# Seven output stores of an attention-and-gate kernel, issued by SyncE instead of ScalarE

## The chip, the core and the metric

The kernel runs on one core of a Trainium2 chip. The metric is the device time of one execution in microseconds (us), the median of several runs. The engines are named as in the profile: PE is TensorE (PEld its weight loads), ACT is ScalarE, DVE is VectorE, POOL is GpSimd, SP is SyncE. SP does no arithmetic here: it only issues DMA transfers. A name with a q behind it (SPq, ACTq) is the instruction queue of that engine, in which DMA-issuing instructions stand. DMA-issuing instructions are not counted as busy time of their engine.

## What is computed

Two steps, for 8 batches, 8 heads, 576 positions and a head width of 64. The first is causal attention in blocks of 64 (a position sees its own block and all earlier ones); the second gates a linear layer with a causal convolution over 5 positions and multiplies by an output matrix.

```python
scores = scale * np.matmul(q, k.transpose(0, 1, 3, 2))
scores = np.where(block_i >= block_j, scores, -1e9)
attn = softmax(scores)
x = (attn @ v).transpose(0, 2, 1, 3).reshape(B, S, H * D)      # 8 x 576 x 512
gate = sigmoid(sum over k of conv_w[k] * x shifted by 4 - k)
out = (gate * (x @ w_val)) @ w_out                             # 8 x 576 x 512, fp32
```

## The kernel before

**Order written by hand.** The whole program is a list of words, `PLAN`, and a loop (L643) that reads them one after the other and calls one small function for each. A word is `name/arguments/engine/PSUM banks`: `E/20.0/A` is the function `E` with arguments 20 and 0 on ACT, `S/20.0/P/6+7` is `S` on PE into PSUM banks 6 and 7. The engine letters are P (PE), A (ACT), V (DVE), G (POOL) and S (SP). No scheduler reorders them: on each engine the instructions stand in the order of the words. A layer below adds the semaphores: what an instruction waits for follows from the tiles that it reads and writes.

**The attention.** A unit `k` is four heads' worth of q or k, a pair `p` (0 to 31) is two heads. `lQ` loads q or k into the fp32 tiles `st`, `lv` and `lvt` load v into `vs` and `vts`; SP issues all of these loads. `c` casts a unit to fp16, `T` transposes it on PE, `Te` copies the transposed unit out of PSUM into `qkT`. `S` multiplies q by k into two PSUM banks, `E` (ACT, L395) takes the exponential of them into the tile `pt`, `mka` and `mkb` (POOL, L415) set the masked corner of `pt` to zero, `cv` casts v (POOL or DVE) into `v16`, `A` multiplies `pt` by v, `N` (DVE) divides by the sum of the row into `x16`. `SL`, `EL`, `AT` and `NT` do the same for the last 64 positions. `X` and `XT` transpose the result and `Xe`, `XTe` copy it into `xt`.

**The gate.** `C` is the convolution on PE, `CS` (ACT) its tanh, `V` the product with `w_val`, `Ve` (DVE) multiplies the two into `gv`, `O` multiplies 128 rows of `gv` by `w_out` into one PSUM bank.

**The output.** `Oe` copies such a 128 x 512 block from PSUM into one of six buffers `osb` (`NOSB`, L129), on ACT (L228) or on DVE (L230). `Od` (L614, L615) stores it to `out`, 256 KB in one DMA. The buffers are used in turn in the order of the `Oe` words, so the copy number n + 6 waits until the store of copy n has landed.

```python
    DMA = {"S": nc.sync, "A": nc.scalar}                       # L224

    def Od(u, t, eng, bank=None):                              # L614
        DMA[eng].dma_start(out=rows(u, t), in_=outs[u, t][0:128])
```

The letter in an `Od` word therefore says which engine issues the store: `S` puts it among the loads in SP's queue, `A` among the exponentials and copies in ACT's queue. Of the 35 stores of `osb`, SP issues 24 and ACT 11. Every DMA reports its landing on one of eight semaphores, which are dealt out in turn and used again; before a DMA is issued, its issuer waits until the DMA that had this semaphore before has landed. The listings below call them DMAHW0 to DMAHW7.

Of the kernel before, what the change touches and what calls it, by code (L numbers as in the profile page):

```python
# [65 lines left out]
C/4/P/0+1+4+5 T/22/P/2+3 CS/4.1/A CS/4.0/A O/1.4/P/6 S/20.2/P/4+5 E/20.2/A Te/22/V Oe/1.4/V  # L66
lQ/14.1.0/S Od/0.5/S lv/20.0/S lQ/12.1.1/S AT/4/P/7 S/21.0/P/0+1 T/23/P/2+3 S/21.1/P/4+5 E/21.0/A
E/21.1/A O/1.1/P/6 Oe/1.1/A NT/4/V Te/23/V A/16/P/0+1 S/23.2/P/2+3 S/22.2/P/4+5 E/22.2/A A/17/P/6+7
E/23.2/A cv/22/G mkb/18/G lQ/14.0.0/S lv/21.1/S lQ/13.0.1/S Od/1.4/A lQ/13.0.0/S lQ/13.1.1/S
lv/23.1/S lv/20.1/S lv/23.0/S lv/27.1/S c/25/G cvt/6/G c/24/G N/16/V N/17/V V/4.3/P/0 A/19/P/4+5  # L70
Ve/4.3/V S/20.0/P/6+7 X/8/P/2+3 E/20.0/A Xe/8/A A/18/P/0+1 N/19/V XT/4/P/4 O/1.2/P/5 N/18/V XTe/4/V
S/23.0/P/6+7 SL/5/P/2+3 S/20.1/P/0+1 Oe/1.2/V X/9/P/4 V/4.2/P/5 E/23.0/A EL/5/A Xe/9/V Ve/4.2/V
# [1 line left out]
T/24/P/2+3 S/22.0/P/0+1 S/23.1/P/6+7 E/22.0/A E/23.1/A lQ/13.1.0/S lvt/5/S Od/1.0/S lQ/14.0.1/S  # L74
cv/21/G lv/26.1/S lv/24.0/S mkb/23/G cv/20/G mkb/22/G mka/21/G mkb/21/G mka/20/G mka/23/G c/29/G
Ve/5.3/V Ve/4.0/V Te/24/V O/1.3/P/5 V/5.2/P/4 Oe/1.3/V S/22.1/P/2+3 E/22.1/A T/26/P/0+1 S/24.2/P/6+7
E/24.2/A Od/0.7/A V/5.0/P/5 Ve/5.2/V Te/26/V A/20/P/2+3 cvt/5/G mka/22/G c/27/G S/24.1/P/0+1
S/24.0/P/6+7 E/24.1/A E/24.0/A Ve/5.0/V cv/23/G N/20/V V/4.1/P/5 lv/25.1/S lQ/15.1.1/S lQ/15.1.0/S
lv/26.0/S Od/1.1/S lv/25.0/S lv/27.0/S Ve/4.1/V V/5.1/P/4 S/25.0/P/0+1 E/25.0/A T/27/P/2+3
S/25.2/P/6+7 AT/5/P/5 A/21/P/0+1 E/25.2/A Ve/5.1/V Te/27/V NT/5/V N/21/V S/25.1/P/2+3 A/22/P/4+5  # L80
O/1.6/P/6 E/25.1/A N/22/V S/27.2/P/2+3 T/29/P/0+1 S/27.1/P/4+5 Te/29/V Oe/1.6/A E/27.2/A E/27.1/A
O/2.1/P/6 XT/5/P/7 XTe/5/A Oe/2.1/V mkb/24/G mkb/25/G cv/26/G lv/28.1/S lQ/15.0.1/S lQ/15.0.0/S
lv/31.1/S lv/24.1/S Od/1.2/S Od/2.1/A A/23/P/2+3 X/10/P/0+1 S/27.0/P/4+5 E/27.0/A O/1.5/P/7 N/23/V
Xe/10/V S/26.2/P/2+3 X/11/P/0+1 S/26.1/P/4+5 cv/25/V Xe/11/V O/2.2/P/6 E/26.2/A Oe/1.5/A E/26.1/A
C/6/P/0+1+2+3 cv/27/V Oe/2.2/V c/30/V cv/24/V c/28/G c/31/G Od/1.3/S lv/30.0/S Od/2.2/S lv/30.1/S
lv/28.0/S Od/1.5/S lv/31.0/S lvt/7/S Od/1.6/S CS/6.0/A CS/6.1/A T/28/P/4+5 Te/28/V V/6.0/P/6
# [9 lines left out]
mkb/29/G Ve/7.0/V S/30.1/P/0+1 S/30.0/P/2+3 S/31.2/P/4+5 E/30.1/A E/30.0/A mka/30/G E/31.2/A  # L96
mkb/31/G V/7.2/P/7 V/7.3/P/6 A/29/P/0+1 Ve/7.2/V A/30/P/2+3 Ve/7.3/V O/3.0/P/4 A/28/P/6+7 N/30/V
N/29/V N/28/V A/31/P/2+3 N/31/V O/2.8/P/5 AT/7/P/6 X/15/P/2+3 X/14/P/0+1 NT/7/V Xe/14/V O/2.4/P/7
XT/7/P/6 XTe/7/V Oe/2.4/V Xe/15/A Oe/3.0/A Oe/2.8/A Od/2.8/A C/8/P/0+1+2+3 C/9/P/4+5+6+7 CS/8.0/A
Od/2.5/A CS/9.1/A Od/2.6/A CS/8.1/A Od/2.4/A CS/9.0/A Od/3.0/S Od/2.3/S V/9.2/P/0 V/8.3/P/1  # L100
V/8.0/P/6 V/8.1/P/7 V/8.2/P/2 V/9.3/P/3 V/9.0/P/4 V/9.1/P/5 Ve/8.0/V Ve/8.3/V Ve/8.1/V Ve/8.2/V
O/3.3/P/2 O/3.1/P/1 Ve/9.2/V Ve/9.1/V Ve/9.3/V Ve/9.0/V Oe/3.1/V Oe/3.3/A Od/3.3/A Od/3.1/S
O/3.4/P/2 Oe/3.4/A Od/3.4/A O/3.2/P/4 Oe/3.2/V OL/0/P/2 OL/1/P/3 OLe/0/V Od/3.2/A OLe/1/V OLd/0/A
# [593 lines left out]
```

## Time and profile before

| what | us |
| --- | --- |
| median of 3 runs | 179.41 |
| lowest and highest of these runs | 178.64 and 180.15 |
| the profiled execution, its own time | 180.11 |
| the span of the profiled execution | 178.2 |
| PE busy in that span | 164.5 |
| ACT busy | 136.8 |
| DVE busy | 129.1 |
| POOL busy | 71.6 |

The span runs from the first to the last instruction of the profiled execution; 1.91 us of its own time lie around it. All times in the views are counted from the start of the span. In a row of the timeline stand the start, the length, the engine, the line of the kernel, the operation, the tile written and the tile read, the number of instructions of that kind in a row (x2), and in brackets how long the engine stood idle before it and which engine, by the profile, ended that wait.

### The profile page before, as it was taken

How to read it: one execution, taken by the hardware profiler on the slowest of the kernel's cores; microseconds unless marked ns; L12 is line 12 of the kernel's file. 1: busy time of each engine (PE TensorE's matmuls, PEld its weight loads, DVE VectorE, ACT ScalarE, POOL GpSimd, SP SyncE). 2: the span in 40 equal slices, each digit the busy share in tenths (PEclk: the TensorE clock that was granted, in tenths of full speed). 3: DMA queues.
4: the chain of work that ended last, by engine and by line, in shares of the span. 5: the costliest groups of instructions: out<-in, count | busy, mean ns of one | idle time of the engine just before them, and what ended most of it. 6: DMA issues, size and time to landing. Idle time of an engine off the chain costs nothing.

```text
span 178.2 us, 7667 instructions
## 1 busy us (share of the span) xinstructions
PE 164.5 (92%) x3292; PEld 95.2 (53%) x3292; DVE 129.1 (72%) x238; ACT 136.8 (77%) x161; POOL 71.6 (40%) x149
## 2 busy tenths in 40 slices
PE   7688789989999999999999969999999999999991
PEld 2233565565454765666546635565553755755450
DVE  4478997576879889985768847988994846744730
ACT  3388999985799889998999498887887699065142
POOL 6233664827557557573373810654103053000000
PEclk9999999999999999999999999999999999999999
DMA  6999979999989999999999999157476200045085
GB/s 190 332 353 266 266 204 298 216 311 310 349 179 304 297 295 246 352 332 339 280 257 302 264 299 276 67 132 227 136 185 212 81 4 4 0 165 197 21 307 204
DMA packets 53692, 40.35 MB, mean 226 GB/s; under 512 B 39701, under 2 KB 39957, under 8 KB 53658
## 3 DMA queue, kind: packets, MB, share of 16 engines
q1 hardware_dynamic: 51930, 36.85, 71.8%
q10 hardware_dynamic: 1728, 3.02, 4.5%
q8 instruction: 25, 0.41, 1.1%
q14 instruction: 9, 0.07, 0.1%
HBM read 30.42 MB, written 9.44 MB: 224 GB/s over the span
## 4 chain that ended last, share of the span: by engine, by line
PE 68%; DVE 12%; DMA 5%; issue 4%; ACT 4%; SPq 3%; POOL 3%; POOLq 0%; ACTq 0%; DVEq 0%
PE PS L135 60%; PE PS L139 7%; DVE qkT L230 3%; DMA st<-in_k_dram 3%; DVE gv L577 2%; DMA out_dram<-osb 2%; DVE qk L230 2%; ACT pt L395 2%; POOL pt L415 1%; DVE x L447 1%; DVE w_val L230 1%; SPq L264 1%; ACT th L559 1%; SPq L258 1%; DVE xt L230 1%
## 5 line engine op out<-in xcount | busy, mean ns | idle before, releaser
L395 ACT ACTIVATE pt<-PS 128x1024 f16<-128x1024 f32 x96 | 93.0, 1030 | 9.0 <-PE PS L135 8.0
L230 DVE COPY qkT<-PS 128x1152 f16<-128x1152 f16 (+1 forms) x29 | 38.7, 1334 | 6.8 <-PE PS L139 6.7
L415 POOL MEMSET pt<- 64x256 f16 x64 | 20.9, 348 | 46.5 <-ACT pt L395 36.6
L577 DVE SCALAR_TENSOR_TENSOR gv<-th,PS 128x112 f16<-128x112 f32 (+4 forms) x64 | 26.1, 449 | 17.7 <-PE PS L135 14.9
L135 PE MATMUL PS<-qkT 64*128 64x64 f16 (+4 forms) x384 | 36.1, 277 | 2.8 <-ACT pt L395 1.4
L135 PE MATMUL PS<-xt,w_val 128*128 128x464 f16 x160 | 35.7, 360 | 0.5 <-ACT osb L228 0.4
L135 PE MATMUL PS<-w_out,gv 128*128 128x512 f16 (+1 forms) x148 | 35.6, 374 | 0.0
L135 PEld LDWEIGHTS <-pt 128*128 128x128 f16 (+1 forms) x960 | 27.7, 102 | 8.6 <-issue 4.0
L135 PE MATMUL PS<-v,pt 128*128 128x65 f16 (+1 forms) x896 | 30.7, 194 | 1.3 <-DVE x L447 0.8
L230 POOL CAST qk<-st 128x1152 f16<-128x1152 f32 (+1 forms) x23 | 25.7, 1128 | 13.8 <-DMA st<-in_q_dram 4.9
L447 DVE TENSOR_TENSOR x<-PS,rc 128x512 f16<-128x512 f32 x32 | 22.1, 692 | 1.3 <-DVE rc L446 0.2
L135 PEld LDWEIGHTS <-qkT 64*128 64x128 f16 x384 | 13.1, 94 | 17.7 <-issue 12.6
L135 PEld LDWEIGHTS <-w_val 128*128 128x128 f16 x160 | 13.9, 97 | 15.8 <-issue 3.9
L559 ACT ACTIVATE th<-PS 128x928 f32<-128x928 f32 x20 | 17.8, 946 | 5.1 <-PE PS L135 5.1
L230 POOL CAST v<-vs 128x512 f16<-128x512 f32 x26 | 15.9, 617 | 11.8 <-issue 6.8
L135 PEld LDWEIGHTS <-gv 128*128 128x128 f16 x148 | 12.7, 98 | 13.3 <-issue 2.2
L228 ACT COPY osb<-PS 128x512 f32<-128x512 f32 x18 | 10.5, 590 | 10.9 <-PE PS L135 7.7
L139 PE MATMUL PS<-ident,qk 64*128 64x64 f16 x576 | 13.7, 190 | 3.1 <-DVE qk L230 2.2
L139 PEld LDWEIGHTS <-qk 64*128 64x128 f16 x576 | 11.5, 95 | 9.0 <-DVE qk L230 3.3
L135 PE MATMUL PS<-xt,DG 32*32 32x464 f16 x800 | 13.1, 358 | 0.9 <-DVE xt L230 0.4
L230 DVE COPY osb<-PS 128x512 f32<-128x512 f32 x17 | 11.7, 686 | 2.5 <-PE PS L135 1.9
L230 DVE COPY xt<-PS 128x1024 f16<-128x1024 f16 (+1 forms) x15 | 8.7, 583 | 5.6 <-PE PS L139 5.6
(49 smaller groups left out, 103.5 us busy)
## 6 DMA issues: line engine op xcount, KB each, us to landing
st<-in_q_dram SPq DMA_DIRECT2D x32, 288.0 KB, 5.4
st<-in_k_dram SPq DMA_DIRECT2D x32, 288.0 KB, 5.2
vs<-in_v_dram SPq DMA_DIRECT2D x64, 128.0 KB, 5.1
out_dram<-osb SPq DMA_DIRECT2D x24, 256.0 KB, 3.4
out_dram<-osb ACTq DMA_DIRECT2D x11, 256.0 KB, 2.4
vts<-in_v_dram SPq DMA_DIRECT2D x8, 128.0 KB, 4.9
gv<-in_moe_w_val_dram SPq DMA_DIRECT2D x2, 512.0 KB, 6.9
osb<-in_moe_w_out_dram SPq DMA_DIRECT2D x2, 512.0 KB, 5.7
```

The costliest lines, as they stand in the source:

```text
L135: made.append(nc.tensor.matmul(out=out, lhsT=lhsT, rhs=rhs, start=start, stop=stop, skip_group_check=True))
L139: made.append(nc.tensor.transpose(out=out, in_=in_, identity=identity))
L228: i = nc.scalar.copy(out=out, in_=in_)
L230: i = (nc.vector if eng == "V" else nc.gpsimd).tensor_copy(out=out, in_=in_)
L258: DMA[eng].dma_start(out=rot(vs, p)[0:128, 0:4, h, 0:64], in_=v[b, 4 * w + 2 * h + r, 0:512, 0:64].rearrange("(c p) d -> p c d", p=128))
L264: DMA[eng].dma_start(out=vts[b % 2][32:96, 0:8, 0:64], in_=v[b, 0:8, 512:576, 0:64].rearrange("h s d -> s h d"))
L395: made.append(nc.scalar.activation(out=rot(pts, p)[0:128, 0:2, 512 * t:512 * t + 512], in_=both(take("S", p, t)), func=AF.Exp, bias=0.0, s ...
L415: nc.gpsimd.memset(rot(pts, p)[64:128, 0:2, a:a + 2 * step].rearrange("p h (t s) -> p h t s", t=2)[:, :, :, 0:64], 0.0)
L447: made.append(nc.vector.tensor_tensor(out=rot(x16, p // 2)[0:128, 0:4, 0:2, p % 2].rearrange("p i h d -> p h i d"), in0=r[:, :, :, 0:64], ...
L559: made.append(nc.scalar.activation(out=rot(ths, n)[0:128, 2 * i:2 * i + 2], in_=both(take("C", n, i))[:, :, 0:RUN], func=AF.Tanh, bias=0.0 ...
L577: made.append(nc.vector.scalar_tensor_tensor(out=gv[0:128, x, a - 4 * i:e - 4 * i], in0=rot(ths, n)[0:128, x, a - o:e - o], scalar=1.0, in ...
```

## The change

The engine letter of seven `Od` words is changed from `A` to `S`: `Od/1.4`, `Od/0.7` and `Od/2.1` in mid-run, and `Od/2.8`, `Od/2.5`, `Od/2.6` and `Od/2.4` shortly before the last two convolutions. Their places in the list of words stay as they are, and nothing else is changed. Five `A` letters stay: `Od/3.3`, `Od/3.4`, `Od/3.2`, `Od/2.7` and `OLd/0`. Two of the changed lines:

```diff
-E/23.2/A cv/22/G mkb/18/G lQ/14.0.0/S lv/21.1/S lQ/13.0.1/S Od/1.4/A lQ/13.0.0/S lQ/13.1.1/S
+E/23.2/A cv/22/G mkb/18/G lQ/14.0.0/S lv/21.1/S lQ/13.0.1/S Od/1.4/S lQ/13.0.0/S lQ/13.1.1/S
-Od/2.5/A CS/9.1/A Od/2.6/A CS/8.1/A Od/2.4/A CS/9.0/A Od/3.0/S Od/2.3/S V/9.2/P/0 V/8.3/P/1
+Od/2.5/S CS/9.1/A Od/2.6/S CS/8.1/A Od/2.4/S CS/9.0/A Od/3.0/S Od/2.3/S V/9.2/P/0 V/8.3/P/1
```

PE's, DVE's and POOL's instructions stand as before; ACT loses seven DMA issues and SP gains them. The first place is ACT's queue around `Od/1.4`. The rows are `E/22.2` and `E/23.2` (into `pt_4` and `pt_5`), the store, `E/20.0` (into `pt_2`) and `Xe/8` (into `xt`); in brackets stand the semaphores that each row waits for.

```order
 L395 ACTIVATE pt_4_110<-PS_63 128x2x512 [waits PE_49,Activation_49,Pool_49]
 L395 ACTIVATE pt_5_111<-PS_63 128x2x512 [waits DVE_49,PE_49]
-L615 DMA out_0_dram<-osb_127 128x512 [waits DMAHW4_49]
 L395 ACTIVATE pt_2_108<-PS_63 128x2x512 [waits DVE_49,PE_49]
 L228 COPY xt_122<-PS_63 128x2x512 [waits PE_49]
```

The store, and with it a wait for the DMA semaphore DMAHW4, is gone from between `E/23.2` and `E/20.0`. The second place is SP's queue at the same words. Before, the rows are `lQ/13.0.1`, `lQ/13.0.0` (into `st_2`), `lQ/13.1.1` (into `st_3`), `lv/23.1`, `lv/20.1`, `lv/23.0` and `lv/27.1`.

```order
L251 DMA st_2_79<-in_q_dram 128x576 [waits DMAHW7_49]
L251 DMA st_2_79<-in_q_dram 128x576 [waits DMAHW0_49]
L251 DMA st_3_80<-in_k_dram 128x576 [waits DMAHW1_49]
L258 DMA vs_3_86<-in_v_dram 128x4x64 [waits DMAHW2_49,Pool_49]
L258 DMA vs_0_83<-in_v_dram 128x4x64 [waits DMAHW3_49]
L258 DMA vs_3_86<-in_v_dram 128x4x64 [waits DMAHW4_49]
L258 DMA vs_2_85<-in_v_dram 128x4x64 [waits DMAHW5_49,Pool_49]
```

After the change the store `Od/1.4` stands second in the same stretch of SP's queue:

```order
L251 DMA st_2_79<-in_q_dram 128x576 [waits DMAHW7_49]
L615 DMA out_0_dram<-osb_127 128x512 [waits DMAHW0_49,DVE_49]
L251 DMA st_2_79<-in_q_dram 128x576 [waits DMAHW1_49]
L251 DMA st_3_80<-in_k_dram 128x576 [waits DMAHW2_49]
L258 DMA vs_3_86<-in_v_dram 128x4x64 [waits DMAHW3_49,Pool_49]
L258 DMA vs_0_83<-in_v_dram 128x4x64 [waits DMAHW4_49]
L258 DMA vs_3_86<-in_v_dram 128x4x64 [waits DMAHW5_49]
L258 DMA vs_2_85<-in_v_dram 128x4x64 [waits DMAHW6_49,Pool_49]
```

The store brings a wait for DVE (its copy `Oe/1.4`) into SP's queue, and the loads behind it move on by one semaphore. The third place is the end of SP's queue, from `Od/1.8` (first row) over `Od/3.0` before, or `Od/2.8` after, to `Od/3.1` and `OLd/1`.

```order
 L615 DMA out_0_dram<-osb_127 128x512 [waits DMAHW1_49,DVE_49]
 L615 DMA out_0_dram<-osb_127 128x512 [waits DMAHW2_49,Activation_49]
-L615 DMA out_0_dram<-osb_127 128x512 [waits DMAHW4_49]
+L615 DMA out_0_dram<-osb_127 128x512 [waits DMAHW3_49,DVE_49]
+L615 DMA out_0_dram<-osb_127 128x512 [waits DMAHW4_49,DVE_49]
+L615 DMA out_0_dram<-osb_127 128x512 [waits DMAHW5_49,DVE_49]
+L615 DMA out_0_dram<-osb_127 128x512 [waits DMAHW6_49]
+L615 DMA out_0_dram<-osb_127 128x512 [waits DMAHW7_49]
 L615 DMA out_0_dram<-osb_127 128x512 [waits DMAHW1_49,DVE_49]
 L628 DMA out_0_dram<-olast_1_76 128x256 [waits DMAHW4_49,DVE_49]
```

The four late stores now go out one behind the other ahead of `Od/3.0` and `Od/2.3`, and the four rows that ACT had between its tanh instructions are gone.

More of the change, by code (lines that the diff above doesn't have):

```diff
@@ L76 @@
 Ve/5.3/V Ve/4.0/V Te/24/V O/1.3/P/5 V/5.2/P/4 Oe/1.3/V S/22.1/P/2+3 E/22.1/A T/26/P/0+1 S/24.2/P/6+7
-E/24.2/A Od/0.7/A V/5.0/P/5 Ve/5.2/V Te/26/V A/20/P/2+3 cvt/5/G mka/22/G c/27/G S/24.1/P/0+1
+E/24.2/A Od/0.7/S V/5.0/P/5 Ve/5.2/V Te/26/V A/20/P/2+3 cvt/5/G mka/22/G c/27/G S/24.1/P/0+1
 S/24.0/P/6+7 E/24.1/A E/24.0/A Ve/5.0/V cv/23/G N/20/V V/4.1/P/5 lv/25.1/S lQ/15.1.1/S lQ/15.1.0/S
@@ L82 @@
 O/2.1/P/6 XT/5/P/7 XTe/5/A Oe/2.1/V mkb/24/G mkb/25/G cv/26/G lv/28.1/S lQ/15.0.1/S lQ/15.0.0/S
-lv/31.1/S lv/24.1/S Od/1.2/S Od/2.1/A A/23/P/2+3 X/10/P/0+1 S/27.0/P/4+5 E/27.0/A O/1.5/P/7 N/23/V
+lv/31.1/S lv/24.1/S Od/1.2/S Od/2.1/S A/23/P/2+3 X/10/P/0+1 S/27.0/P/4+5 E/27.0/A O/1.5/P/7 N/23/V
 Xe/10/V S/26.2/P/2+3 X/11/P/0+1 S/26.1/P/4+5 cv/25/V Xe/11/V O/2.2/P/6 E/26.2/A Oe/1.5/A E/26.1/A
@@ L98 @@
 N/29/V N/28/V A/31/P/2+3 N/31/V O/2.8/P/5 AT/7/P/6 X/15/P/2+3 X/14/P/0+1 NT/7/V Xe/14/V O/2.4/P/7
-XT/7/P/6 XTe/7/V Oe/2.4/V Xe/15/A Oe/3.0/A Oe/2.8/A Od/2.8/A C/8/P/0+1+2+3 C/9/P/4+5+6+7 CS/8.0/A
-Od/2.5/A CS/9.1/A Od/2.6/A CS/8.1/A Od/2.4/A CS/9.0/A Od/3.0/S Od/2.3/S V/9.2/P/0 V/8.3/P/1
+XT/7/P/6 XTe/7/V Oe/2.4/V Xe/15/A Oe/3.0/A Oe/2.8/A Od/2.8/S C/8/P/0+1+2+3 C/9/P/4+5+6+7 CS/8.0/A
+Od/2.5/S CS/9.1/A Od/2.6/S CS/8.1/A Od/2.4/S CS/9.0/A Od/3.0/S Od/2.3/S V/9.2/P/0 V/8.3/P/1
 V/8.0/P/6 V/8.1/P/7 V/8.2/P/2 V/9.3/P/3 V/9.0/P/4 V/9.1/P/5 Ve/8.0/V Ve/8.3/V Ve/8.1/V Ve/8.2/V
```

## The prediction

> **What bounds the kernel now.** I read the page first, then the windows, the waits of one window, and the timelines of the engines around each of the seven stores.
>
> ```profile
> span 178.2 us, 7667 instructions
> PE 164.5 (92%) x3292; PEld 95.2 (53%) x3292; DVE 129.1 (72%) x238; ACT 136.8 (77%) x161; POOL 71.6 (40%) x149
> vs<-in_v_dram SPq DMA_DIRECT2D x64, 128.0 KB, 5.1
> ```
>
> PE is busy for 92% of the span, so PE is the bound. A saving counts here only where it removes idle time of PE, or of an engine for which PE waits. The windows show where PE is idle between the first and the last moved store:
>
> ```profile
> core 0: us, PE busy (x) PEld busy (x) DVE busy (x) ACT busy (x) POOL busy (x), PEclk, DMA share, GB/s
> 100.00:105.00 5.00, 3.20 (x60) 1.95 (x58) 2.84 (x7) 2.34 (x4) 2.46 (x7) 1.00 1.04 259
> 105.00:125.00 20.00, 20.00 (x406) 11.60 (x402) 16.91 (x26) 16.99 (x20) 7.74 (x12) 1.00 0.66 191
> 125.00:138.00 13.00, 12.64 (x263) 6.60 (x263) 10.27 (x19) 10.67 (x15) 2.05 (x7) 1.00 0.59 173
> 138.00:158.00 20.00, 20.00 (x481) 12.89 (x480) 14.33 (x36) 13.63 (x17) 4.32 (x11) 1.00 0.07 22
> ```
>
> PE is busy in every microsecond of 100 to 158 but for two holes: 1.80 us (5.00 less 3.20) between 100 and 105, and 0.36 us between 125 and 138. The granted clock is 1.00 throughout, so clock plays no part. `Od/1.4` stands in the first hole. ACT and PE there:
>
> ```profile
> 98.08 1.94 ACT L395 ACTIVATE pt<-PS 128x1024 f16<-128x1024 f32 x2 [0.26 <-PE PS L135]
> 102.15 0.43 ACTq L615 DMA_DIRECT2D out_dram<-osb  x1
> 102.68 1.02 ACT L395 ACTIVATE pt<-PS 128x1024 f16<-128x1024 f32 x1 [2.66 <-PE PS L135]
> 103.60 1.01 ACT L228 COPY xt<-PS 128x1024 f16<-128x1024 f16 x1
> 104.49 1.04 ACT L395 ACTIVATE pt<-PS 128x1024 f16<-128x1024 f32 x1
> 105.40 0.62 ACT L410 ACTIVATE pt<-PS 128x512 f16<-128x512 f32 x1
> ```
>
> ```profile
> 99.99 0.39 PE L135 MATMUL PS<-qkT 64*128 64x512 f16 x2
> 100.22 0.40 PE L139 MATMUL PS<-ident,x 64*128 64x64 f16 x16
> 101.63 1.03 PE L135 MATMUL PS<-w_out,gv 128*128 128x512 f16 x4
> 103.75 0.39 PE L135 MATMUL PS<-qkT 64*128 64x512 f16 x2 [1.09 <-ACT pt L395]
> 104.65 0.51 PE L135 MATMUL PS<-qkT 64*128 64x64 f16 x12 [0.51 <-ACT xt L228]
> 106.43 0.37 PE L135 MATMUL PS<-xt,DG 32*32 32x464 f16 x2
> ```
>
> ACT is done with `E/23.2` at 100.02 and starts `E/20.0` at 102.68, 2.66 us later. The profile names PE as the releaser, but the scores that `E/20.0` reads (`S/20.0`, the PE row at 99.99) were complete at 100.38. What stands between is the store at 102.15. Its listing waits for nothing but DMAHW4, and the load that SP issued with DMAHW4 in that stretch is `lv/23.0`:
>
> ```profile
> 96.82 0.55 SPq L258 DMA_DIRECT2D vs<-in_v_dram  x1
> ```
>
> Issued at 96.82, with the median landing time of v loads of 5.1 us, it lands at an estimated 101.9, next to the store's 102.15. So I read the hole as this: the store, whose data were ready at 95.05 (DVE row below), held ACT's queue until an unrelated load had landed, and `E/20.0` and `Xe/8` behind it were late for PE, which needs their PSUM banks for `S/23.0` and `SL/5`.
>
> **The change, part by part.** *Store `Od/1.4` off ACT.* `E/20.0` can start at about 100.42, when its scores are there, instead of 102.68; `Xe/8` 0.92 later (102.68 to 103.60), at 101.34 to 102.35. PE then reaches `S/23.0` behind `O/1.2` with its bank free. The two idle times are 1.09 and 0.51, together 1.60. A row's modelled end overlaps its successor by 0.16 (99.99 plus 0.39 against 100.22), so each hole hides another 0.16: 1.60 + 0.32 = 1.92. `S/23.0` would run at 102.50 and `SL/5` at 102.73 instead of 104.65. Next in line is the convolution `C/5`, at 106.43 less 1.92 = 104.51. It needs `EL/5`: `E/23.0` starts when `S/23.0` is complete, 102.9, `EL/5` 0.91 behind it (104.49 to 105.40), done at 104.45. That just fits; nothing of the 1.92 is lost here, but no more than 1.92 can be had either. Lower bound 0.53, the store's own issue and the gap behind it (102.15 to 102.68); upper bound 2.66, ACT's whole idle time. I take 1.92, because it comes from PE's own rows, the bound engine's. From 105 on PE is without a hole but for 0.36, so the gain is carried to the end if nothing else comes too late.
>
> *Stores `Od/0.7` and `Od/2.1` off ACT.*
>
> ```profile
> 112.72 1.02 ACT L395 ACTIVATE pt<-PS 128x1024 f16<-128x1024 f32 x1 [0.27 <-PE PS L135]
> 113.34 0.34 ACTq L615 DMA_DIRECT2D out_dram<-osb  x1
> 123.66 0.34 ACTq L615 DMA_DIRECT2D out_dram<-osb  x1
> 124.13 1.02 ACT L395 ACTIVATE pt<-PS 128x1024 f16<-128x1024 f32 x1 [0.36 <-PE PS L135]
> ```
>
> The issue at 113.34 lies under an exponential that runs to 113.74, past its own end at 113.68: zero. Behind the issue at 123.66 ACT has 0.36 of idle time; its exponential waited for `S/27.0`, so at most 0.1 is the store's. I take zero.
>
> *The four late stores off ACT.*
>
> ```profile
> 158.12 0.34 ACTq L615 DMA_DIRECT2D out_dram<-osb  x1
> 158.56 0.94 ACT L559 ACTIVATE th<-PS 128x928 f32<-128x928 f32 x1 [0.47 <-PE PS L135]
> 160.25 6.44 PE L135 MATMUL PS<-xt,w_val 128*128 128x464 f16 x32
> ```
>
> ACT's tanh waits there for a convolution of PE, and PE runs on from 160.25 for 6.44 us without a gap. Between 0 and 0.47 (the idle time at 158.56); I take zero, since the bound engine does not wait for ACT.
>
> *The same stores on SP.* Each costs 0.33 to 0.43 of SP's queue, some 2.6 in all, and what its waits cost the loads behind it.
>
> ```profile
> 93.11 0.98 SPq L251 DMA_DIRECT2D st<-in_q_dram  x2
> 94.37 0.68 DVE L230 COPY osb<-PS 128x512 f32<-128x512 f32 x1
> 101.67 0.62 POOL L230 CAST v<-vs 128x512 f16<-128x512 f32 x1 [0.51 <-DMA vs<-in_v_dram]
> 102.34 0.81 POOL L415 MEMSET pt<- 64x256 f16 x3
> 106.99 0.31 POOL L415 MEMSET pt<- 64x256 f16 x1 [3.84 <-ACT pt L395]
> 109.46 1.15 ACT L228 CAST qk<-st 128x1152 f16<-128x1152 f32 x1
> 113.88 0.77 PE L135 MATMUL PS<-v,pt 128*128 128x65 f16 x20
> ```
>
> `Od/1.4` reaches the head of SP's queue at 93.6, after the first of the two q loads, and its copy ends at 95.05: SP is held 1.4, plus 0.43 of issue, and the loads behind are issued up to 1.9 later. They also share the DMA engines (share 1.00) with 256 KB more, 1.0 us at the 259 GB/s of that window, so they land at most 2.9 late, and not below zero. The one cast that already waits for such a load is `cv/20` at 101.67. Behind it POOL needs 0.62 and 0.81 and then stands idle for 3.84, until `E/20.1` is done. That comes 1.6 earlier in the changed kernel, which leaves 2.2 of cover against 2.9: at worst one memset is 0.7 late, and its reader `A/20` stands at 113.88, some 6 us behind. Cost zero, at worst some tenths. `c/26` on ACT (109.46), the next reader of these loads, has time for over 5 us of lateness: `lQ/13.0.0` is issued at about 95.5 and c/26 comes at 107.5.
>
> ```profile
> 107.21 9.99 SPq L258 DMA_DIRECT2D vs<-in_v_dram  x3
> 121.26 1.70 SPq L615 DMA_DIRECT2D out_dram<-osb  x2
> 125.53 0.39 SPq L258 DMA_DIRECT2D vs<-in_v_dram  x1
> 132.13 0.62 SPq L615 DMA_DIRECT2D out_dram<-osb  x1
> 135.62 0.58 ACT L228 COPY osb<-PS 128x512 f32<-128x512 f32 x1 [1.18 <-DMA out_dram<-osb]
> ```
>
> `Od/0.7` joins the queue ahead of the stretch at 107.21, in which SP waits for most of 9.99 us for a buffer anyway: covered. `Od/2.1` stands between the two stores at 121.26; its copy is ready when ACT issues it now (123.66), so SP is held to about 124.1, ahead of the load at 125.53 that waits for DVE in any case: covered by 1.4. The late four are followed by stores only, whose buffers are copied into again behind PE's 6.44 us from 160.25: covered.
>
> The sum is −1.92. Against the profiled execution that is 180.11 − 1.92 = 178.2, a span of 176.3. The profiled execution is 0.70 above the median of the runs shown, so the median becomes 179.41 − 1.92 = 177.5.
>
> [...] ACT's idle time holds 2.13 us of waiting ahead of the store and 0.53 of issue. [...]
>
> **The rivals.**
>
> *Issue time alone.* If the profile is right that PE released `E/20.0`, the wait stays and only 0.53 goes: 178.9. For it speaks the releaser named; against it that PE's row had ended 2.3 us earlier. Chance 0.08.
>
> *The gain is partly given back.* PE has no slack to hide a late input in 105 to 158, and `C/5` comes out within 0.1 of its last input. If a cast, a DVE copy or a load becomes the bound there, some 0.6 to 1.2 of the 1.92 is left: 178.2 to 178.8. Against it: every engine waits for PE, not PE for them, in these rows. Chance 0.20.
>
> *Slower: SP's queue becomes the bound at `Od/1.6`.* ACT's copy at 135.62 already waits 1.18 for the store that SP issues at 132.13, and PE's hole of 0.36 hangs on it. Each microsecond by which SP comes later to this store is a microsecond of PE. This starts when `Od/2.1` holds SP past the load at 125.53, so when it is over 1.4 later than I reckon; to end slower it must cost over 1.92 more than that. With 3 us in its place: 179.41 − 1.92 + 3 = 180.5. Chance 0.10, since mishaps of that size upstream (loads landing 5 us late) count here too.
>
> **How the numbers follow.** My forecast, the hole at 100 to 105 closed, has 0.62. About 1% (1.8 us) is what a measurement of this kernel can tell from no change, and 177.5 lies just beyond it: 0.46 of the 0.62 is faster by over 1%, since half of its spread of 1.5 to 2.7 and the chance of a longer wait in other executions lie there. The rest, 0.16, the issue alone and the partial gain (0.28), and none of the slower case, are within 1%: 0.44. Slower by over 1% is 0.10. The range runs from ACT's whole 2.66 (176.7) to no gain at all (179.4), and leaves the slower case and a little on the other side out.
>
> **What would show it.** In the changed profile the windows should give PE near 5.0 of 5.0 in 100 to 105; `E/20.0` should start within 0.5 of `E/23.2`'s end; the store `Od/1.4` should be issued by SP at about 95.1, with a wait for DVE's copy; the 0.36 at 125 to 138 should stay; the rest of PE should be the same rows about 1.9 earlier. I am wrong if ACT still idles over 2 us there, if PE shows a new hole behind a load or behind POOL, or if the wait for `Od/1.6` grows.

## The result, and the profile after

| | median us (lowest to highest) | executions |
|---|---|---|
| before, beside it | 181.03 (178.64 to 185.0) | 22 |
| changed | 178.67 (176.57 to 181.54) | 22 |

The ratio of changed to before is 0.9888, 95% interval 0.9855 to 0.9921: about 1.1% faster. The prediction of −1.92 on 179.41 is a ratio of 0.9893. The changed median is 1.2 us above the predicted 177.5 and inside its range; before itself measured 1.6 above the median that the prediction started from. The ratios, here and below, leave out executions that took over 1.5% longer than the fastest of their kernel, while the medians and ranges are of all executions. The execution that was profiled for the changed kernel is its longest (181.54 us): it had lost 2.56 us ahead of the change, where PE stood idle for 1.81 us and then ran at half its clock for 3.4 us. So I compare inside the stretch of the change, and with a second profile of the same kernel further down. First the head of that page, and its windows. The columns are as in the prediction, with a stretch of the half clock (30 to 40) added:

```profile
span 179.5 us, 7673 instructions
PE 165.8 (92%) x3292; PEld 95.5 (53%) x3292; DVE 128.9 (72%) x238; ACT 137.1 (76%) x161; POOL 72.0 (40%) x149
```

```profile
core 0: us, PE busy (x) PEld busy (x) DVE busy (x) ACT busy (x) POOL busy (x), PEclk, DMA share, GB/s
30.00:40.00 10.00, 9.33 (x171) 4.82 (x170) 5.97 (x10) 8.99 (x11) 6.50 (x12) 0.85 0.82 231
100.00:105.00 5.00, 4.77 (x95) 3.39 (x94) 3.96 (x9) 4.10 (x5) 2.58 (x6) 1.00 0.99 237
105.00:125.00 20.00, 19.98 (x414) 11.65 (x412) 16.94 (x28) 16.76 (x20) 9.04 (x16) 1.00 0.72 203
125.00:138.00 13.00, 12.56 (x262) 6.47 (x261) 10.53 (x18) 10.51 (x13) 2.05 (x7) 1.00 0.62 185
138.00:158.00 20.00, 20.00 (x420) 12.59 (x418) 14.38 (x35) 13.64 (x17) 4.32 (x11) 1.00 0.11 36
```

Between 100 and 105 PE is busy for 4.77 of 5.00 us, where it was 3.20. The 0.36 between 125 and 138 has stayed, as 0.44. The granted clock of 0.85 between 30 and 40 is where time was lost; the moved stores all come later. ACT around the place, in the changed kernel (start, length, instruction, and in brackets the idle time before it with its releaser):

```profile
100.64 1.94 ACT L395 ACTIVATE pt<-PS 128x1024 f16<-128x1024 f32 x2 [0.27 <-PE PS L135]
103.22 1.02 ACT L395 ACTIVATE pt<-PS 128x1024 f16<-128x1024 f32 x1 [0.64 <-PE PS L135]
...
108.75 1.78 ACT L559 ACTIVATE th<-PS 128x928 f32<-128x928 f32 x2 [0.44 <-PE PS L135]
```

The last row begins with `CS/5.1`. Before, that was:

```profile
107.79 0.94 ACT L559 ACTIVATE th<-PS 128x928 f32<-128x928 f32 x1 [0.86 <-PE PS L135]
```

`E/22.2` with `E/23.2` comes 2.56 us later than before (98.08 to 100.64), and `CS/5.1` only 0.96 later (107.79 to 108.75): 1.60 us were won between them. The idle time before `E/20.0` is 0.64 instead of 2.66, a little over the 0.5 that the prediction named. The end of the span keeps what was won here, less 0.3 us at a second place that comes and goes (told further down): 179.5 against 178.2 is 1.3 later.

The second profile of the changed kernel, taken with the experiments, has a span of 175.9 and stands at before's times up to this place, so that its rows compare directly. ACT, and then PE:

```profile
98.10 1.94 ACT L395 ACTIVATE pt<-PS 128x1024 f16<-128x1024 f32 x2 [0.27 <-PE PS L135]
100.45 1.02 ACT L395 ACTIVATE pt<-PS 128x1024 f16<-128x1024 f32 x1 [0.41 <-PE PS L135]
...
104.03 0.59 ACT L410 ACTIVATE pt<-PS 128x512 f16<-128x512 f32 x1
105.98 1.78 ACT L559 ACTIVATE th<-PS 128x928 f32<-128x928 f32 x2 [0.44 <-PE PS L135]
```

```profile
100.01 0.39 PE L135 MATMUL PS<-qkT 64*128 64x512 f16 x2
101.64 1.03 PE L135 MATMUL PS<-w_out,gv 128*128 128x512 f16 x4
102.59 0.72 PE L135 MATMUL PS<-qkT 64*128 64x512 f16 x14
104.67 1.27 PE L135 MATMUL PS<-xt,DG 32*32 32x464 f16 x80
```

`S/20.0` is at 100.01 (99.99 before). `S/23.0` and `SL/5`, which began at 103.75 and 104.65 and had idle time before each, are one row at 102.59 without any, and `C/5` begins at 104.67 instead of 106.43. That is 1.78 us on PE, since `S/20.0` itself is 0.02 later. On ACT, from 98.10 to 105.98 are 7.88 us where 98.08 to 107.79 were 9.71: 1.83 less.

### The profile page after: what moved, and what is told of

It is laid out like the page before. It is cut to its first block, busy times and chain, and to the rows that moved or that the text cites. A ratio compares the mean times of both kernels' runs of the same rounds, so it can differ in the third digit from the quotient of the medians.

```text
span 179.5 us, 7673 instructions
## 1 busy us (share of the span) xinstructions
PE 165.8 (92%) x3292; PEld 95.5 (53%) x3292; DVE 128.9 (72%) x238; ACT 137.1 (76%) x161; POOL 72.0 (40%) x149
## 3 DMA queue, kind: packets, MB, share of 16 engines
q10 hardware_dynamic: 720, 1.18, 1.8%
## 4 chain that ended last, share of the span: by engine, by line
PE 68%; DVE 9%; ACT 6%; DMA 6%; issue 4%; POOL 3%; SPq 2%; POOLq 0%; ACTq 0%; DVEq 0%
PE PS L135 60%; PE PS L139 7%; ACT pt L395 4%; DVE qkT L230 3%; DMA st<-in_k_dram 3%; DMA out_dram<-osb 3%; DVE gv L577 2%; ACT th L559 2%; POOL pt L415 1%; DVE x L447 1%; DVE qk L230 1%; SPq L258 1%; SPq L251 1%; ACT osb L228 1%; POOL qk L230 1%
## 5 line engine op out<-in xcount | busy, mean ns | idle before, releaser
L415 POOL MEMSET pt<- 64x256 f16 x64 | 21.5, 358 | 46.6 <-ACT pt L395 36.8
L135 PEld LDWEIGHTS <-DG 32*32 32x32 f16 x800 | 9.4, 89 | 5.8 <-issue 4.0
```

The lines of the kernel that those rows point to most:

```text
L135: made.append(nc.tensor.matmul(out=out, lhsT=lhsT, rhs=rhs, start=start, stop=stop, skip_group_check=True))
L415: nc.gpsimd.memset(rot(pts, p)[64:128, 0:2, a:a + 2 * step].rearrange("p h (t s) -> p h t s", t=2)[:, :, :, 0:64], 0.0)
```

## The experiments

The theory to be tested: on ACT the store `Od/1.4` waits at the head of an in-order queue for a semaphore that an unrelated load still holds, and that wait, not the issue, costs PE 1.8 us. The rivals are the issue time alone (PE, as the profile says, releases `E/20.0`), and, for what is left of the time, that SP's queue with one store more makes its loads late.

### One store alone, and the other six alone

The first kernel moves `Od/1.4` alone from ACT to SP; the edit is against before:

```diff
-E/23.2/A cv/22/G mkb/18/G lQ/14.0.0/S lv/21.1/S lQ/13.0.1/S Od/1.4/A lQ/13.0.0/S lQ/13.1.1/S
+E/23.2/A cv/22/G mkb/18/G lQ/14.0.0/S lv/21.1/S lQ/13.0.1/S Od/1.4/S lQ/13.0.0/S lQ/13.1.1/S
```

> Only Od/1.4 is issued by SyncE; the other six stores stay on ScalarE. Theory (the one store's semaphore wait is the whole effect): as the full change, 1.5 to 2.1 us under the kernel before, ratio about 0.989; ACT's idle time ahead of E/20.0 falls from 2.66 to under 0.7 us, PE idle between E/20.0's scores and the convolution C/5 falls from 1.6 to 0.2 us or less. Rival (all seven count, each by its issue of 0.34 to 0.43): about 0.5 us under the kernel before.

Measured: 177.97 us (177.41 to 178.38, 9 executions), ratio to before 0.9903, interval 0.9868 to 0.9938. The rows are those of the changed kernel:

```profile
97.95 1.94 ACT L395 ACTIVATE pt<-PS 128x1024 f16<-128x1024 f32 x2 [0.26 <-PE PS L135]
100.30 1.02 ACT L395 ACTIVATE pt<-PS 128x1024 f16<-128x1024 f32 x1 [0.41 <-PE PS L135]
105.85 1.78 ACT L559 ACTIVATE th<-PS 128x928 f32<-128x928 f32 x2 [0.44 <-PE PS L135]
```

From 97.95 to 105.85 are 7.90 us: one store carries the whole gain. The opposite edit, again against before, moves the other six and leaves `Od/1.4` on ACT:

```diff
-E/24.2/A Od/0.7/A V/5.0/P/5 Ve/5.2/V Te/26/V A/20/P/2+3 cvt/5/G mka/22/G c/27/G S/24.1/P/0+1
+E/24.2/A Od/0.7/S V/5.0/P/5 Ve/5.2/V Te/26/V A/20/P/2+3 cvt/5/G mka/22/G c/27/G S/24.1/P/0+1
...
-lv/31.1/S lv/24.1/S Od/1.2/S Od/2.1/A A/23/P/2+3 X/10/P/0+1 S/27.0/P/4+5 E/27.0/A O/1.5/P/7 N/23/V
+lv/31.1/S lv/24.1/S Od/1.2/S Od/2.1/S A/23/P/2+3 X/10/P/0+1 S/27.0/P/4+5 E/27.0/A O/1.5/P/7 N/23/V
...
-XT/7/P/6 XTe/7/V Oe/2.4/V Xe/15/A Oe/3.0/A Oe/2.8/A Od/2.8/A C/8/P/0+1+2+3 C/9/P/4+5+6+7 CS/8.0/A
-Od/2.5/A CS/9.1/A Od/2.6/A CS/8.1/A Od/2.4/A CS/9.0/A Od/3.0/S Od/2.3/S V/9.2/P/0 V/8.3/P/1
+XT/7/P/6 XTe/7/V Oe/2.4/V Xe/15/A Oe/3.0/A Oe/2.8/A Od/2.8/S C/8/P/0+1+2+3 C/9/P/4+5+6+7 CS/8.0/A
+Od/2.5/S CS/9.1/A Od/2.6/S CS/8.1/A Od/2.4/S CS/9.0/A Od/3.0/S Od/2.3/S V/9.2/P/0 V/8.3/P/1
```

> The other six stores are issued by SyncE, Od/1.4 stays on ScalarE. Theory: no gain; the hole at E/20.0 stays. By the order the store shares its semaphore now with the load one place further on (lv/27.1 instead of lv/23.0), which lands some 0.5 us later, so the hole may grow by about 0.5: time equal to the kernel before or up to 0.6 us above it. Rival (the six others carry part of the gain): 0.5 to 1.5 us under the kernel before, with the hole at E/20.0 unchanged.

Measured: 181.39 us (178.69 to 185.38, 12), ratio 1.0025, interval 0.9974 to 1.0077. ACT:

```profile
97.96 1.94 ACT L395 ACTIVATE pt<-PS 128x1024 f16<-128x1024 f32 x2 [0.26 <-PE PS L135]
101.23 0.37 ACTq L615 DMA_DIRECT2D out_dram<-osb  x1
101.71 1.02 ACT L395 ACTIVATE pt<-PS 128x1024 f16<-128x1024 f32 x1 [1.81 <-PE PS L139]
106.83 1.78 ACT L559 ACTIVATE th<-PS 128x928 f32<-128x928 f32 x2 [0.86 <-PE PS L135]
```

The hole stays and nothing is gained: the six are worth nothing, as reckoned. The hole is 1.81 us and not as long as before's 2.66; I had expected it to grow. In this kernel the store shares its semaphore with `lv/27.1` instead of `lv/23.0`, and SP issued that load at 96.36, earlier than before's `lv/23.0` at 96.82, and it landed faster: 4.85 us from issue to landing (96.36 to 101.21), as against 5.30 (96.82 to 102.12). So in these two profiles the length of the hole follows the load, not the store. From 97.96 to 106.83 this execution needs 8.87 us, 0.84 less than before's 9.71; the median of the 12 doesn't show that as a gain.

### The store stays on ACT, at two other places

If the wait counts and the issue does not, a store on ACT is harmless where its semaphore is free, and harmful where it is not. Both kernels move only the one word, on before, and all stores of ACT stay on ACT. First behind `E/20.1`:

```diff
-E/23.2/A cv/22/G mkb/18/G lQ/14.0.0/S lv/21.1/S lQ/13.0.1/S Od/1.4/A lQ/13.0.0/S lQ/13.1.1/S
+E/23.2/A cv/22/G mkb/18/G lQ/14.0.0/S lv/21.1/S lQ/13.0.1/S lQ/13.0.0/S lQ/13.1.1/S
...
-C/5/P/2+3+6+7 E/20.1/A CS/5.1/A CS/5.0/A T/25/P/0+1 Te/25/V V/5.3/P/5 V/4.0/P/4 c/26/A mkb/20/G
+C/5/P/2+3+6+7 E/20.1/A Od/1.4/A CS/5.1/A CS/5.0/A T/25/P/0+1 Te/25/V V/5.3/P/5 V/4.0/P/4 c/26/A mkb/20/G
```

> As the kernel before, all seven stores on ScalarE, but Od/1.4 stands behind E/20.1, four ACT operations later. There it shares its semaphore with the load lv/24.0, issued 6 us later than lv/23.0. Theory (the wait counts, wherever it stands): E/20.0 starts at once, the hole moves to the tanh of C/5 (CS/5.1), which starts 2 us or more late, until lv/24.0 has landed; PE stands idle there for 1.5 us or more, and the time is within 0.5 us of the kernel before. Rival (what the profile names, PE, or only the place of the issue counts): no hole of over 0.6 us on ACT at either place, 0.5 to 1.9 us under the kernel before.

Measured: 179.6 us (177.75 to 183.09, 12), ratio 0.9947, interval 0.9896 to 0.9999. ACT, then PE's longest wait between 96 and 160 (total, times, longest):

```profile
100.47 1.02 ACT L395 ACTIVATE pt<-PS 128x1024 f16<-128x1024 f32 x1 [0.41 <-PE PS L135]
...
108.38 0.38 ACTq L615 DMA_DIRECT2D out_dram<-osb  x1
108.81 1.78 ACT L559 ACTIVATE th<-PS 128x928 f32<-128x928 f32 x2 [3.24 <-DMA vs<-in_v_dram]
```

```profile
PE PS L139 <- ACT th L559: 2.6, 1, 2.6
```

The hole has gone from before `E/20.0` (0.41) and stands behind `E/20.1`, 3.24 us long, and here the profile itself names a load of v as the releaser of a tanh that reads nothing of v. The time was expected within 0.5 us of before; by the ratio it is 1.0 us under it. In the list of words that load, `lv/24.0`, stands behind the store: the layer deals the semaphores out in an order of its own, not in that of the words. The same kernel once more:

> The kernel with Od/1.4 behind E/20.1 on ScalarE once more: its profile showed ACT held 3.24 us by the load that shares the store's semaphore, PE idle 2.6 us, and a granted clock of 0.50 for 3.4 us behind that, but its median was 0.5% under the kernel before. Theory: the wait is real in every execution and the half clock only in some; the profile shows a hole of 2 to 3.5 us on ACT ahead of CS/5.1 again, and where the clock stays at 1.0 the rows behind the hole come within 1 us of those of the kernel before. Rival (the hole was an accident of one execution): no hole over 1 us.

Measured: 180.25 us (177.8 to 184.51, 13), ratio 1.0082, interval 1.0026 to 1.0138. The hole was there again, and longer than the 2 to 3.5 us expected:

```profile
111.19 0.37 ACTq L615 DMA_DIRECT2D out_dram<-osb  x1
111.62 1.78 ACT L559 ACTIVATE th<-PS 128x928 f32<-128x928 f32 x2 [6.09 <-DMA vs<-in_v_dram]
```

PE waited 5.5 us for it, and behind that its clock was at 0.50 for 3.4 us again (by the windows 0.80 in 110 to 115 and 0.93 in 115 to 125), so what happens at the full clock wasn't seen. The wait is where the theory puts it, but its length differs between executions, from 3.24 to 6.09 us, and the two times, 0.9947 and 1.0082, differ by more than their intervals allow. The second place is two exponentials further, behind `E/23.1` (against before):

```diff
-E/23.2/A cv/22/G mkb/18/G lQ/14.0.0/S lv/21.1/S lQ/13.0.1/S Od/1.4/A lQ/13.0.0/S lQ/13.1.1/S
+E/23.2/A cv/22/G mkb/18/G lQ/14.0.0/S lv/21.1/S lQ/13.0.1/S lQ/13.0.0/S lQ/13.1.1/S
...
-T/24/P/2+3 S/22.0/P/0+1 S/23.1/P/6+7 E/22.0/A E/23.1/A lQ/13.1.0/S lvt/5/S Od/1.0/S lQ/14.0.1/S
+T/24/P/2+3 S/22.0/P/0+1 S/23.1/P/6+7 E/22.0/A E/23.1/A Od/1.4/A lQ/13.1.0/S lvt/5/S Od/1.0/S lQ/14.0.1/S
```

> As the kernel before, all seven stores on ScalarE, but Od/1.4 stands behind E/23.1, some 8 us later; the load that shares its semaphore (lv/24.0) has then landed. Theory (the wait counts, the issue itself is cheap): as the full change, 1.5 to 2.1 us under the kernel before, although no store has left ScalarE; the issue of some 0.4 us hides beside the exponentials. Rival (it is the issuing on ScalarE that costs): no more than 0.5 us under the kernel before.

Measured: 177.74 us (176.77 to 178.93, 11), ratio 0.9907, interval 0.9868 to 0.9946.

```profile
97.92 1.94 ACT L395 ACTIVATE pt<-PS 128x1024 f16<-128x1024 f32 x2 [0.26 <-PE PS L135]
100.27 1.02 ACT L395 ACTIVATE pt<-PS 128x1024 f16<-128x1024 f32 x1 [0.41 <-PE PS L135]
105.81 1.78 ACT L559 ACTIVATE th<-PS 128x928 f32<-128x928 f32 x2 [0.45 <-PE PS L135]
108.52 1.04 ACT L395 ACTIVATE pt<-PS 128x1024 f16<-128x1024 f32 x1
108.66 0.37 ACTq L615 DMA_DIRECT2D out_dram<-osb  x1
```

The store is issued by ACT, under the exponential that runs from 108.52 to 109.56, and costs nothing: from 97.92 to 105.81 are 7.89 us, as with the store on SP. ACT issues as many stores as before, and the gain is the same. The load on the store's semaphore is `lv/24.0` here too, but by the trace it had landed at 106.69, 1.97 us ahead of the store. That settles it against the issue time.

The trace's records of landings say the same. In the four executions in which ACT waited, the store was issued within 0.03 us of the landing of a load on its own semaphore:

| kernel | load, issued | landed | store issued |
|---|---|---|---|
| before | `lv/23.0`, 96.82 | 102.12 | 102.15 |
| other six alone | `lv/27.1`, 96.36 | 101.21 | 101.23 |
| behind `E/20.1` | `lv/24.0`, 103.76 | 108.36 | 108.38 |
| the same again | `lv/24.0`, 104.94 | 111.17 | 111.20 |

### The changed kernel again, and the store at other places of SP's queue

> The changed kernel once more, as the measure for the three kernels beside it. 1.5 to 2.1 us under the kernel before; E/20.0 starts within 0.7 us of E/23.2's end.

Measured: 178.54 us (176.74 to 181.04, 12), before beside it 179.83, ratio 0.9973, interval 0.9922 to 1.0024. By this ratio the gain is 0.5 us, by the medians 1.3, both short of the 1.5 to 2.1 expected, while the rows, shown above, have the whole gain. Whoever goes by this ratio alone would call the change nothing. SP's queue and one wait of POOL in this run:

```profile
95.10 0.34 SPq L615 DMA_DIRECT2D out_dram<-osb  x1
95.49 0.93 SPq L251 DMA_DIRECT2D st<-in_q_dram  x1
```

```profile
102.60 0.62 POOL L230 CAST v<-vs 128x512 f16<-128x512 f32 x1 [2.13 <-DMA vs<-in_v_dram]
...
105.59 0.31 POOL L415 MEMSET pt<- 64x256 f16 x1 [1.51 <-ACT pt L395]
```

The store leaves SP at 95.10, right behind its DVE copy, and the q load behind it goes at 95.49 instead of 93.66, 1.83 later. `cv/20` on POOL starts at 102.60 instead of 101.67, 0.93 later, and POOL still idles 1.51 us before it is needed. To see if the 1.83 us cost anything, one kernel puts the store behind six of the loads, and one puts it so early that SP stands still for its copy. The first (against the changed kernel):

```diff
-E/23.2/A cv/22/G mkb/18/G lQ/14.0.0/S lv/21.1/S lQ/13.0.1/S Od/1.4/S lQ/13.0.0/S lQ/13.1.1/S
-lv/23.1/S lv/20.1/S lv/23.0/S lv/27.1/S c/25/G cvt/6/G c/24/G N/16/V N/17/V V/4.3/P/0 A/19/P/4+5
+E/23.2/A cv/22/G mkb/18/G lQ/14.0.0/S lv/21.1/S lQ/13.0.1/S lQ/13.0.0/S lQ/13.1.1/S
+lv/23.1/S lv/20.1/S lv/23.0/S lv/27.1/S Od/1.4/S c/25/G cvt/6/G c/24/G N/16/V N/17/V V/4.3/P/0 A/19/P/4+5
```

> The changed kernel with Od/1.4 five loads later in SP's queue (behind lv/27.1), so that SP meets it when its copy is long done. Theory (the 1.4 us by which SP is held for the copy are covered): the same as the changed kernel within 0.3 us; SP's loads behind lQ/13.0.1 are issued 1 to 2 us earlier and nobody on PE's path starts earlier for it. Rival (the loads held back cost part of the gain): 0.4 to 1 us under the changed kernel.

Measured: 178.25 us (176.26 to 179.07, 12), ratio to before 0.9949, interval 0.9900 to 0.9998. The idle time before `E/20.0` is 0.41, as in the changed kernel, and PE's rows have gained nothing more behind it: from `S/20.0` at 99.06 to `C/5` at 103.73 are 4.67 us, as against 4.66. The second, with the store right behind `Od/0.5` (against the changed kernel):

```diff
-lQ/14.1.0/S Od/0.5/S lv/20.0/S lQ/12.1.1/S AT/4/P/7 S/21.0/P/0+1 T/23/P/2+3 S/21.1/P/4+5 E/21.0/A
+lQ/14.1.0/S Od/0.5/S Od/1.4/S lv/20.0/S lQ/12.1.1/S AT/4/P/7 S/21.0/P/0+1 T/23/P/2+3 S/21.1/P/4+5 E/21.0/A
...
-E/23.2/A cv/22/G mkb/18/G lQ/14.0.0/S lv/21.1/S lQ/13.0.1/S Od/1.4/S lQ/13.0.0/S lQ/13.1.1/S
+E/23.2/A cv/22/G mkb/18/G lQ/14.0.0/S lv/21.1/S lQ/13.0.1/S lQ/13.0.0/S lQ/13.1.1/S
```

> The changed kernel with Od/1.4 six DMAs earlier in SP's queue (behind Od/0.5), so that SP is held for the copy some 4 us instead of 1.4. Theory (loads have about 5 us of time before their readers, POOL's casts about 2): the casts on POOL come up to 3 us late, PE loses at most 0.5 us, time within 0.5 us of the changed kernel. Rival (SP's lateness reaches PE one for one): 2.5 us over the changed kernel, slower than the kernel before.

Measured: 178.05 us (176.32 to 179.34, 12), ratio 0.9933, interval 0.9881 to 0.9984. SP, POOL, and the windows:

```profile
91.34 4.15 SPq L615 DMA_DIRECT2D out_dram<-osb  x2
```

```profile
99.99 1.15 POOL L230 CAST qk<-st 128x1152 f16<-128x1152 f32 x1 [6.06 <-DMA st<-in_k_dram]
```

```profile
100.00:105.00 5.00, 4.80 (x107) 2.99 (x104) 3.86 (x9) 3.85 (x6) 4.02 (x6) 1.00 1.12 292
105.00:125.00 20.00, 20.00 (x418) 11.34 (x386) 17.50 (x28) 17.14 (x20) 9.59 (x17) 1.00 0.85 241
```

SP's two stores take 4.15 us, with a wait that holds the loads behind them, POOL waits 6.06 us for a load of k and makes this cast 4.6 us later than in the changed kernel's second profile (99.99 against 95.39), and PE is as busy as in the changed kernel's second profile: 4.80 of 5.00 (there 4.81) and 20.00 of 20.00. The cover for late loads is deep at this place, and no difference between either kernel and the changed one is shown.

### The small hole at 125 to 138

The prediction left one PE hole of 0.36 us, and blamed the store `Od/1.6`. Here it is moved ahead of the seven words of SP that stood before it (against the changed kernel):

```diff
-C/6/P/0+1+2+3 cv/27/V Oe/2.2/V c/30/V cv/24/V c/28/G c/31/G Od/1.3/S lv/30.0/S Od/2.2/S lv/30.1/S
-lv/28.0/S Od/1.5/S lv/31.0/S lvt/7/S Od/1.6/S CS/6.0/A CS/6.1/A T/28/P/4+5 Te/28/V V/6.0/P/6
+C/6/P/0+1+2+3 cv/27/V Oe/2.2/V c/30/V cv/24/V c/28/G c/31/G Od/1.3/S Od/1.6/S lv/30.0/S Od/2.2/S lv/30.1/S
+lv/28.0/S Od/1.5/S lv/31.0/S lvt/7/S CS/6.0/A CS/6.1/A T/28/P/4+5 Te/28/V V/6.0/P/6
```

> The changed kernel with Od/1.6 right behind Od/1.3 in SP's queue, six DMAs earlier; its copy is ready there. Theory (PE's hole of 0.36 at 125 to 138 hangs on the landing of this store through the copy Oe/1.7): ACT's wait for the store, 1.18 before, is gone, the hole is gone, 0.3 to 0.5 us under the changed kernel. Rival (the copy waits for its matmuls anyway): no difference, and the hole stays with PE or another releaser.

Measured: 178.05 us (176.9 to 178.63, 12), ratio to before 0.9968, interval 0.9934 to 1.0002. First ACT's copy in the changed kernel's second profile, then the same copy and the window of this kernel:

```profile
133.69 0.58 ACT L228 COPY osb<-PS 128x512 f32<-128x512 f32 x1 [1.06 <-DMA out_dram<-osb]
```

```profile
133.14 0.58 ACT L228 COPY osb<-PS 128x512 f32<-128x512 f32 x1
```

```profile
125.00:138.00 13.00, 13.00 (x282) 7.37 (x281) 10.66 (x21) 10.91 (x15) 1.57 (x6) 1.00 0.64 185
```

The wait of 1.06 us is gone and PE has no hole left there. That alone doesn't show the cause, since the kernel with `Od/1.4` alone on SP leaves `Od/1.6` in its place and PE is busy 13.00 of 13.00 there too. But the profiles of all kernels agree on the length: where this copy waits for the store for 0.50, 0.51 or 0.77 us, PE has no hole, and where it waits for 1.04, 1.18 or 1.26 us, PE's hole is 0.23, 0.36 or 0.44, each time 0.82 or 0.81 less than the wait. So the wait makes the hole, and the earlier store takes the wait away. Set row against row, this kernel is 0.51 us behind the second profile of the changed one ahead of that place and 0.02 ahead of it from 137.4 on: 0.53 us. The medians differ by 0.5 too, but the ratios to before, 0.9968 and 0.9973, do not, so no gain in time is shown.

Both of these edits together, the store `Od/1.4` behind the loads and `Od/1.6` early, on the changed kernel:

> The changed kernel with Od/1.6 behind Od/1.3 and Od/1.4 behind lv/27.1, both on SyncE: the two moves that showed no harm. Theory: PE has no hole over 0.25 us between 100 and 158; 0.3 to 0.5 us under the changed kernel, 2.0 to 2.6 us under the kernel before. Rival: the later landing of Od/1.4 or of the loads opens a new wait, no better than the changed kernel.

Measured: 177.59 us (176.6 to 178.51, 12), before 180.33, ratio 0.9928, interval 0.9889 to 0.9967. PE is busy 13.00 of 13.00 between 125 and 138. It has the lowest median of all that were run, 2.7 us under before by the medians but 1.3 by the ratio, where 2.0 to 2.6 was expected; a lead over the changed kernel is not shown by these runs.

## Why the prediction was right

**The hole at `Od/1.4`: right in its mechanism, a little too large in its size.** `E/20.0` was to start at about 100.42; it started at 100.45 in the second profile. The runs at other places on ACT show that the wait for the semaphore makes the hole, and that the releaser that the profile of before named (PE) was not it: the scores were there 2.3 us earlier, and where the same store waits elsewhere, the profile names the load. The term of the sum was 1.92 us and measured 1.78 on PE, 0.14 less. One mis-sized part is the overlap: I gave each of PE's two idle times 0.16 more, read off one pair of rows. In the second profile `S/23.0` begins at 102.59, and the `O/1.2` before it ends by its row at 101.64 + 1.03 = 102.67, so that overlap is 0.08 and not 0.16. In sum 0.05 of the 0.14 were lost ahead of `C/5`, and 0.09 at `C/5` itself. That the first ratio, 0.9888, comes so near to the forecast 0.9893 is luck: the second one of the same kernel is 0.9973.

**"That just fits" did not quite hold.** The row ahead of `C/5` is `V/4.2`, first before, then in the second profile of the changed kernel:

```profile
105.56 0.95 PE L135 MATMUL PS<-xt,w_val 128*128 128x464 f16 x4
```

```profile
103.71 0.95 PE L135 MATMUL PS<-xt,w_val 128*128 128x464 f16 x4
```

`V/4.2` gained 1.85 us (1.87 with the 0.02 of `S/20.0`), and `C/5` behind it 1.76 (106.43 to 104.67): 0.09 was lost between them. `EL/5` ends at 104.03 + 0.59 = 104.62, not at the 104.45 of the prediction, and `C/5` begins 0.05 behind it, as `S/23.0` of before began 0.05 behind the end of `E/20.0` (102.68 + 1.02 = 103.70, and 103.75), for which it waited. The row shows no idle time in brackets, because by its modelled end `V/4.2` runs to 104.66. So `C/5` did wait for `EL/5`, as the rival of a partial gain had it, but for 0.09 and not for 0.7 or more.

**The other six: zero, as said.** The run with them alone gives 1.0025. The tanh at the place of the four late stores had 0.47 of idle time before and has 0.46 now.

**SP: covered, as said.** The store was to be issued at about 95.1 and was issued at 95.10. Of the 2.9 us by which loads could be late and the 2.2 of cover at `cv/20`, 0.93 was used. That holding SP for 4.15 us reaches POOL and not PE shows that the rival of a slower kernel through SP's queue had no ground at this place. At its own place, `Od/1.6`, the wait was 1.26 in the first profile and 1.06 in the second, against 1.18 before, and the hole stayed.

**Issue and wait.** Of ACT's 2.66 us before, 0.53 are the issue and the gap behind it, and the gain is 1.78 on PE. With 0.37 to 0.38 us of issue on ACT, the same store costs nothing behind `E/23.1` and 3.24 or 6.09 us of ACT behind `E/20.1`. By the table of landings the rest is a wait that ends with a load's landing, here for stores that ACT issues.

**The rivals.** Issue time alone falls with the store that stays on ACT at no cost. Of the partial gain the rows show the 0.09 at `C/5`. No kernel with the store on SP was slower than before.

**What stays open.** One more PE hole, late in the program, is not the same in all runs. Before, PE's row of the last 55 matmuls of the convolution, and ACT's tanh behind it:

```profile
159.31 1.00 PE L135 MATMUL PS<-xt,DG 32*32 32x464 f16 x55 [0.42 <-issue]
```

```profile
160.35 0.94 ACT L559 ACTIVATE th<-PS 128x928 f32<-128x928 f32 x1 [0.85 <-PE PS L135]
```

The hole of 0.42 is 0.69 in the first profile of the changed kernel, whose tanh at this place comes at 161.65, 1.30 later than before, where the one ahead of it was 1.02 later (159.58 against 158.56). It is absent in the second, where the two come at 156.62 and 158.06. Over all kernels it lies between none and 0.75, without a pattern that I found; the profile gives "issue" as its releaser, which names nothing. So of the 2.3 us between the spans 178.2 and 175.9, 1.8 is the hole at `Od/1.4`, 0.1 the smaller hole at 125 to 138 (0.36 to 0.25), and 0.4 this one, which the two profiles of the changed kernel have at 0.69 and not at all, so that it can't be put down to the change.

Open also is why the ratios of kernels without the hole lie between 0.9888 and 0.9973, although each has the same 1.8 us in its rows. The record shows that it is mostly the kernel before that moves: the executions that the ratios use average 179.6, 178.9 and 178.3 us for it in the three rounds of experiments, and between 177.6 and 178.2 for every kernel without the hole. By the medians of all executions these kernels are 1.3 to 2.9 us under before. A kernel with the hole pays for a load's landing, and that differs from execution to execution (1.81 to 6.09 us of ACT in the four above), so before's own time moves. That it moves by enough to explain these ratios is argued, not shown: only one execution of before was profiled.

## What to carry to other kernels

Where DMAs share their semaphores as here, a DMA that is issued from a busy engine's queue brings along a wait for whatever transfer had its semaphore before, and everything behind it on that engine waits too (here ACT, idle for 1.81 to 6.09 us, with the store issued within 0.03 us of that landing); look at what that transfer is and when it lands, not at the time of issue. Where the profile names a releaser that had been done long before (by 2.3 us here), look for a DMA issue between the two rows. Such a store may as well stay on its engine and be moved a few words, to a place where its semaphore is free and an instruction of the engine runs on over it, as behind `E/23.1`, where ACT needed 7.89 us for the stretch, as with the store on SP (7.88 and 7.90); at another place, as behind `E/20.1`, the wait was longer (3.24 and 6.09 us of ACT, as against 2.66).

## What the hardware showed that I had not expected

In three of the profiles PE's granted clock fell to 0.50, each time behind a hole of PE: of 1.81, 2.63 and 5.5 us. Behind the 2.63 us of the run with the store behind `E/20.1`, the windows of one microsecond each were (columns as above, the granted clock third from the end):

```profile
110.00:111.00 1.00, 0.36 (x20) 0.36 (x21) 0.96 (x2) 1.00 (x2) 0.00 (x0) 1.00 1.12 350
111.00:112.00 1.00, 1.00 (x12) 0.34 (x5) 0.82 (x1) 1.00 (x2) 0.00 (x0) 0.51 0.90 253
112.00:113.00 1.00, 1.00 (x3) 0.30 (x2) 0.54 (x1) 1.00 (x2) 0.00 (x0) 0.50 0.29 70
```

By the clock's records it is 0.50 for 3.4 us (111.0 to 114.4), so by an estimate from these two figures the hole of 2.6 us costs up to 1.7 more. The first profile of the changed kernel shows the same 3.4 us at 0.50 (29.6 to 33.0) behind a hole of 1.81 us (26.6 to 28.4, released by "issue", cause open). Before's two holes of 1.09 and 0.51 left the clock at 1.00.

By its record in the trace, the dip of the first profile of the changed kernel is 3.413 us long. The dips do not begin at once behind a hole, but 7, 31 and 31 times that length behind the first entry of the clock's records (5.74 to 29.64 in the first profile of the changed kernel, 5.21 to 111.02 and 7.16 to 112.98 in the two of the store behind `E/20.1`). The records of the full clock have such lengths too: 23.893 and 146.773 us in the first profile of the changed kernel and 174.080 in before's are 7, 43 and 51 times 3.4133.

Laid out on that grid from its first entry on, the stretches of 3.413 us just ahead of the three dips held 1.81, 2.63 and 3.41 us of idle time of PE. The hole of 5.5 us, of which the 3.41 are a part, had put 1.59 into the stretch before, and that one was followed by the full clock. So was every other stretch within the span of the first profile of the changed kernel, with at most 1.07 us of idle time, and every one within before's, with at most 1.43; the one with the hole at `Od/1.4` held 1.28. The other nine profiled executions have mean granted clocks of 0.996 to 1.000, these three 0.990, 0.988 and 0.987. So in these profiles a hole was followed by a dip where 1.81 us or more of it fell into one such stretch, and was not where 1.59 or less did; between the two nothing was measured.

One dip takes 0.01 off the mean clock of an execution (half of 3.4 in 178): the first profile of the changed kernel, with one, has 0.990. A mean of 0.991 or less was recorded in 34 of the 89 executions of before beside the experiments and in 11 of the 37 of the kernels that keep the hole, but in 1 of the 80 of those without it. That the hole at `Od/1.4` lowered the clock in these executions of before is likely, but not shown: none of them was profiled.
